# Another written-out order for a BigBird-attention and MLP kernel: loads, transposes and the mask's table at other places

## The chip, the cores and the metric

The kernel runs on one core of one Trainium2 chip. Its time is the device time of one execution in microseconds (us); the time of the kernel before is the median of three runs.

## The reference

Attention over 4 batches, 8 heads, 768 positions and head size 64, with a block mask (blocks of 32: neighbours, the first and last block, three drawn blocks for each row), and behind it a residual MLP that first mixes positions and then channels:

```python
scores = scale * q @ k.T                     # per batch and head, 768 x 768
scores = where(mask, scores, -1e9)           # block mask from sampled_blocks
attn = softmax(scores); x = attn @ v         # heads side by side: (4, 768, 512)

a1 = alpha1 * x + beta1
u  = x + lam * (w_tok @ a1)                  # mix of positions
a2 = alpha2 * u + beta2
ch = maximum(a2 @ w_ch1, 0) @ w_ch2          # 512 -> 2048 -> 512
out = u + lam * ch
```

## The kernel before

Nothing in this kernel is scheduled by a planner at build time. The whole order of work is a string, `ORDER`, of 1,589 words (line 49 and following). Each word is a kind, a number and sometimes an argument; the loop at the end calls the function registered for the kind. `pin_order` then ties the instructions of each engine to the order in which they were issued, and `bank_order` adds the waits that the eight banks of PSUM need. So every engine works strictly in the order of the words that fall to it, and a word that waits holds up everything behind it on its engine:

```python
for word in ORDER.split():
    kind = word[: next(j for j, c in enumerate(word) if c.isdigit())]
    n, _, arg = word[len(kind) :].partition(":")
    step[kind](int(n), *args)
```

Attention runs over 16 pairs of heads, p = 0 to 15, and each pair over 9 units of 1,024 scores (n = 9p to 9p + 8). The words of the attention are:

- `lq`, `lk`, `lv` p: POOL issues the load of a pair's q, k or v (192 KB as moved), which go through six shared buffers. From pair 7 on, the load first waits for a flag that a word `F` sets on DVE.
- `cq`, `ck`, `cv` p: copies of a loaded tile into the layout needed, on ACT (`:a`) or DVE (`:d`); they free the load's buffer.
- For the pairs 0 to 4, `H` transposes a head's q and k on TensorE, and `hq`, `hk` copy the result. From pair 5 on, `tq` and `tk` p let SP issue a DMA transpose of q or k (L593).
- `q` n:j: the scores of unit n on TensorE (L624 for the first five pairs, L634 after); `e` n: the exponential on ACT (L645); `m` n: the mask by a minimum on DVE, from pair 5 on; `p`, `r` n: the values on TensorE (L661); `n`, `nt`: normalising on DVE (L709, L712).

For the first five pairs the mask is part of the contraction. For the others a table `maskT` is needed: `M0` writes 24 rows of it from a tile of the mask on DVE (L532), `N0` lets SP write these rows to memory, spread out (L538), and `O0` reads the table back in its final shape (L545).

The words of the MLP are:

- `lt` g: thirds of w_tok (384 KB each); `W`, `w`: its transposes on TensorE and their copies; `k`: the mix of positions (L763); `a`, `b`, `ah`, `bh`, `x`, `u`, `U`, `v` around it.
- `lw` g and `lx` g: the four quarters of w_ch1 and of w_ch2 (512 KB each); `lc`: the small vectors. w_ch2 takes the place in SBUF that w_tok had.
- `f` i:bank: one column group of the first half of the MLP on TensorE, four matmuls (L828) into a PSUM bank; `g` i: bias and relu out of that bank, on ACT or DVE (L842, L844).
- `S` g: scales an eighth of w_ch2 by lam, on DVE (L513); S0 and S1 need lx0, S2 and S3 lx1, S4 and S5 lx2, S6 and S7 lx3. `T`: sums of quarters of w_ch2 on DVE (L866).
- `A`, `h`, `o`: the second half (a scheme with seven products in place of eight); `V`, `Y`, `y`, `d`, `D`: the first half for the later batches; `P` scales w_ch1; `s`: stores.
- `z`: matmuls that fill time on TensorE and compute nothing.

All loads are issued by POOL, in the order of their words, and go through one DMA queue, q0; the DMA transposes and the mask's writes and reads are issued by SP, in the order of their words, and go through others (q1 in the profile).

Of the kernel before, what the change touches and what calls it, by code (L numbers as in the profile page):

```python
# [54 lines left out]
ck3:d q25:1 F22 w0:d lk5 p12 w5:d e25 p13 q19:3 n2 W4:4 e19 H6:0 F28 lx3 w4:d q22:1 hk6:d r13:1
q17:2 e22 L1 q20:3 hq6:d e17 q24:1 L0 r14 H7:0 e20 q18:2 ck4:d a0 lv3 r15 e18 r16 r17 lc5 b0 q23:3
e24 cv2:d k1:4 n3 lk6 e23 lx1 q21:1 cq4:d r22:1 F42 x1 H9:5 e21 lv6 q28:3 F38 a1 p18:4 lw0 e28 r23
F40 q26:1 b1 p19 e26 hk9:d p20 r24 p21 hq7:d r25 cq6:a q27:3 cv4:d hq9:d r26 lq7 e27 p22 q30:1 hk7:d
k0:5 lw3 n5 e30 lc4 L2 H8:0 F23 F32 x0 q35:3 lw1 hk8:a hq8:d q31:1 lw2 k3:5 n4 e35 lx2 cv3:d q29:0
# [8 lines left out]
g28:a f18:0 cq8:d cv5:d g13:a f22:5 cv7:d tq6 g16:d g6:a f21:2 g23:d g22:a f27:1 g18:a tk8 P3:d  # L68
g20:a g21:d f14:3 g27:a P2:d f29:2 tk7 g14:a F34 b4 lk11 f30:0 g29:d lk9 tq8 cq11:d q53:2 g30:a
q48:1 P4:d k9:1 e53 lk12 A8 A0 lv8 e48 q50:3 q46:2 x9 h0:0 lq10 e46 A9 A1 h14:1 e50 A4 q52:1 o0  # L70
q49:2 e52 q45:3 A2 h1 A10 e49 h2 o12 A11 e45 h15 m48 P0:a F27 m50 lq9 q51:1 q47:2 m49 p48:6 e47 k8:7
F43 m45 m46 e51 p49 p50 o1 q58:2 x8 q56:1 e58 nt16 h16 m51 e56 m52 q60:2 q59:3 h3 o13 e60 A3 p45:2
m58 e59 p46 h17 m53 u8:a m47 u9:a q57:2 q55:3 F36 o2 e57 p47 U4 o14 p51:3 m59 h4 ck11:a m56 p52 e55
p53 nt15 lk14 q63:2 nt17 h18 e63 o3 q64:1 m57 q54:3 e64 q71:2 m60 h5 o15 e54 p57:2 a5 p58 h6 e71 b5
p59 ck12:a m64 q70:2 q62:3 nt19 e70 h19 lk10 m71 e62 q69:1 m54 q61:2 h20 F47 A5 ck9:a m55 p54:6
cq9:a k11:7 lv11 o16 e61 o4 tq9 lq13 h7:1 x11 cq10:a m62 k10:0 tk9 e69 m61 lv9 p60:7 A6 q67:2 tq10
m69 p55 e67 p56 o6 q80:1 x10 p61 e80 p62 nt18 q66:2 h8 nt20 e66 m70 q78:1 ck10:a q68:3 a6 p69:0 e68
p70 lk13 h9 m66 b6 e78 p71 o7 q65:2 q76:3 m63 u10:a q75:1 e65 nt23 h10 m67 u11:a p63:0 cv8:d k12:4
e76 m65 U5 lq12 m68 p66:5 e75 p64 x12 p67 tk10 p68 o8 q81:3 nt22 q86:1 e81 p65 h11 nt21 e86 m75
q74:2 q73:3 a7 e74 k13:0 b7 e73 q72:1 x13 q77:2 o9 u12:a k14:0 u13:a m76 e72 U6 k15:6 x14 A7 e77  # L80
p75:0 p76 x15 q79:1 u14:a m72 q85:2 u15:a h12 m77 e79 U7 m73 p77 e85 q82:3 m80 q93:1 s5 h13 m78 e93
tq11 m79 p78:4 p72:5 m74 e82 p73 p79 tk11 o10 p80 p74 q84:1 P1:d q87:3 nt24 e84 s0 f37:1 m86 tk12
f35:5 e87 nt26 f39:2 ck13:d g35:a m84 lq14 f54:3 g37:a nt25 g39:a q89:2 cv9:d q95:3 e89 q94:0 g54:d
lv10 f38:2 m82 e95 f32:3 P5:d P7:d f34:4 g32:a P6:d f48:5 e94 ck14:d m85 lk15 p84:3 a8 g34:a q83:3
q98:0 e83 p85 cq12:d f47:4 F44 F41 cv11:d tq12 lv15 m81 e98 p86 f61:6 g47:d lv12 g48:a p81:7 m83
q92:0 g61:a q88:2 b8 g38:a p82 f49:6 nt28 e92 m98 f36:2 e88 g49:d f63:3 m89 g36:a q106:0 m87 q91:2
g63:a p83 f51:6 e106 nt27 f56:2 m88 g51:a p87:3 cq13:d e91 f41:7 V0 m94 p88 g56:a q90:0 q96:2 cv10:d
g41:a m93 f52:2 e90 m92 p89 f57:6 m95 g52:a f53:7 e96 V2 p93:2 nt29 g57:a q97:0 q99:2 cq14:d e97
f33:3 m96 tq14 m91 p94 e99 p95 k16:6 m97 tk13 g33:a nt31 g53:a q104:0 m90 q102:1 s2 e104 q103:2 x16
f62:7 s1 a9 e102 tq13 p90:6 p91 p96:0 m99 p92 g62:a p97 nt30 tk14 p98 e103 f60:1 nt32 q113:1 m104  # L90
g60:a q100:2 s3 q105:3 e113 m102 s4 f59:0 b9 k17:1 e100 m113 F45 m103 lq15 e105 f55:2 x17 f44:3 lv14
g59:a m100 g55:a q108:2 m106 q107:0 lv13 e108 q101:3 m105 k18:2 a10 e107 p102:4 f50:5 m108 e101 x18
p99:0 p100 b10 g50:a f58:1 m101 g44:a p103 g58:a q131:3 m107 q115:1 p105:5 A20 e115 f45:1 A12 p106
e131 p104 A16 p101 p107 nt33 g45:a q112:1 k21:6 nt34 e112 nt35 q116:0 A21 q111:1 e116 q130:2 a11
k19:7 e111 x21 h35:0 x19 e130 m111 f43:1 m131 k20:2 g43:a A17 cv12:a o30 q109:2 V4 q114:3 e109 f40:1
A22 f42:3 m112 g40:a f46:4 e114 x20 m109 p111:1 h36 g46:a m114 g42:a cq15:d q110:2 m116 q133:1 e110
q126:3 b11 h37 m115 u16:a p112 ck15:a p113 p114:4 nt37 p115 e126 p116 tk15 p108:5 m130 p109 h28:1
e133 o31 A13 tq15 h38 cv14:a nt38 o24 u20:a q129:1 m110 q127:3 h29 A18 e127 A23 p110 e129 h30 nt36
o32 u21:a q134:2 A19 q132:1 e134 q128:3 o25 h39 m126 u17:a m129 q117:2 e128 U8 h31 m133 u18:a o33
p129:6 u19:a p130 m128 p131 e117 U9 k23:7 a12 e132 h40 o26 U10 nt43 cv15:a h41 x23 b12 u23:a q138:1  # L100
m127 q118:2 q119:3 e118 o34 h32 V5 cv13:a h21:0 m132 e119 m134 k25:4 o27 e138 k24:5 A14 x25 q142:1
o18 q143:3 A15 p126:4 p127 e143 x24 h33 m118 e142 p132:5 m117 h34 m138 p133 o28 p134 q141:1 nt44
q139:3 e141 p117:1 m143 p128 p118 h22 e139 nt42 m119 q135:1 a14 q125:2 e135 k22:6 b14 u24:a p119
e125 x22 h23 m141 u22:a q120:1 nt39 q140:2 e120 q137:3 U11 m142 k29:1 o19 e140 V1 k28:2 m125 u25:a
x29 e137 p141:3 U12 p142 m120 p143 h24 u29:a m139 m140 q123:2 q121:3 o20 e123 p138:1 x28 p139 h25
nt47 e121 Y8 p140 o21 u28:a q124:1 q122:2 e124 q136:3 nt46 U14 h26 Y9 e122 V3 y112:1 p120:2 m121
y126:3 e136 y113:4 Y10 h27 d126:a m135 d112:a m122 y127:5 y119:6 o22 y114 d119:a y120:7 d130 s6 y128
d113:a V6 y121 s10 d127:a p135:0 y115 Y11 d120:a y133:5 d116 d114:a y129 d123 y122 d133:a y117:4
m136 D116:a p121 y116 d128:a d117 p122 y131:7 d121:a nt40 p136 y118 d131 y130 y140:2 m124 d129:a
y123 m137 y135 d115:a y132 d118 d140:a y124:3 d132 p137 d122:a y141:1 d124 D117:a y142 y161:4 d144  # L110
d141:a y162:6 m123 y125 d161:a y134:1 nt45 d134:a y143 d165 y154:7 D130:a y136 d137 d154:a y147:6
d125 p123:0 D124:a p124 a15 D132:a p125 y156 d135:a y163 b15 d147:a y155:1 y148:3 nt41 d142:a y149
d158 y137 y145:0 d151 d148:a k31:1 d145 d162:a V7 d155:a y144 a13 y138:3 d136:a y150 d143:a y157
d138 y164 y146 b13 d149:a y152:2 x31 D158:a y139 D137:d k26:5 u31:a d146 D144:a D145:d d152 d156:a
y159:0 d139 k27:1 d163:a D165:d D151:a x26 D123:a y166:3 x27 y151 y153 d166 u27:a k30:1 D138:d u26:a
d153 D166:a U13 d159 y167 D139:a D125:d y165 D152:a d167 y160 h42:5 D118:d D167:a D131:d d160 D153:a
# [962 lines left out]
```

## Time and profile before

| | |
|---|---|
| median of three runs | 292.2 us (292.03 to 292.49) |
| the profiled execution | 291.82 us, span 290.1 us from the first to the last instruction |
| mean granted TensorE clock | 1.00 |
| TensorE busy | 283.9 us (98%), 3,538 matmuls |
| DVE busy | 263.8 us (91%) |
| ACT busy | 234.0 us (81%) |
| POOL busy | 53.3 us (18%) |
| DMA | 30.95 MB, 107 GB/s over the span |

The profile is of one execution. Rows of a timeline give a start, a duration, the engine, the code line, the operation with the tile written and the tiles read, and in square brackets how long the engine had stood idle before and what released it. Slices show tenths of busy time in 40 equal parts of the span, about 7.25 us each. The names in the rows are those of the program: `rel` a casted q or k, `qx` and `kx` the transposed ones, `eT` a unit's exponentials, `wtk` w_tok, `w1b` and `w2b` the MLP's weights, `hts` the MLP's hidden values, `x_sb` the running result, `psum` a PSUM bank.

### The profile page before, as it was taken

The page shows a single profiled execution, that of the slowest core. Times are in us where ns is not written, and L with a number is a line of the kernel's source. Part 1 is how long each engine was busy: PE and PEld are TensorE (multiplying, and loading weights), DVE is VectorE, ACT ScalarE, POOL GpSimd, SP SyncE. Part 2 cuts the span into 40 slices and gives each one's busy share as a digit, 9 for nine tenths or more (in the row PEclk, how much of TensorE's full clock was granted, in tenths as well). Part 3 has the DMA queues.
Part 4 walks back from the last instruction along what each step waited for, and adds up shares of the span by engine and source line. Part 5 has one row for each costly group of instructions (what it writes and reads, how often), then busy time and mean ns, then how long its engine had stood idle before and what let it go on. Part 6 is the DMA issues. An engine that isn't in the chain of part 4 may idle for free.

```text
span 290.1 us, 8529 instructions
## 1 busy us (share of the span) xinstructions
PE 283.9 (98%) x3538; PEld 213.6 (74%) x3538; DVE 263.8 (91%) x595; ACT 234.0 (81%) x350; POOL 53.3 (18%) x102
## 2 busy tenths in 40 slices
PE   8899999999999999999999999999999999999995
...
DVE  5689997689999999999999999999999998699983
...
PEclk9999999999999999999999999999999999999999
DMA  6999999999983498499278002404110140330014
GB/s 161 189 246 210 195 211 194 203 165 176 168 115 30 53 140 118 74 164 135 27 186 146 7 2 57 85 3 47 37 75 0 19 112 0 148 145 1 2 42 177
DMA packets 47927, 30.95 MB, mean 107 GB/s; under 512 B 28792, under 2 KB 43984, under 8 KB 47888
## 3 DMA queue, kind: packets, MB, share of 16 engines
...
HBM read 31.16 MB, written 6.88 MB: 131 GB/s over the span
## 4 chain that ended last, share of the span: by engine, by line
PE 87%; ACT 5%; DMA 4%; DVE 2%; issue 1%; POOL 0%; ACTq 0%
PE psum L907 26%; PE psum L997 13%; PE psum L828 12%; PE psum L661 11%; PE psum L763 11%; PE psum L634 9%; PE psum L624 4%; DMA wtk<-in_moe_w_tok_dram 3%; ACT hts L842 2%; ACT eT L645 2%; DMA k2f<-in_k_dram 1%; PE psum L806 1%; PE psum L355 1%; DVE a1p L733 0%; ACT rel L419 0%
## 5 line engine op out<-in xcount | busy, mean ns | idle before, releaser
L645 ACT ACTIVATE eT<-psum 128x1024 f16<-128x1024 f32 (+1 forms) x145 | 140.4, 1028 | 9.3 <-PE psum L634 5.4
L655 DVE TENSOR_TENSOR eT<-eT,maskT 128x960 f16<-128x960 f16 x99 | 61.2, 650 | 0.0
L907 PEld LDWEIGHTS <-hts 128*128 128x128 bf16 x480 | 45.1, 98 | 8.5 <-issue 2.1
L661 PEld LDWEIGHTS <-eT 128*128 128x128 f16 x1152 | 44.4, 97 | 8.3 <-issue 1.7
L661 PE MATMUL psum<-vext,eT 128*128 128x65 f16 x1152 | 48.5, 193 | 0.0
L828 PE MATMUL psum<-uT,w1b 128*128 128x384 bf16 (+1 forms) x256 | 45.9, 327 | 0.1
L1023 ACT ACTIVATE snap<-psum,b1t 128x384 f32<-128x384 f32 x44 | 23.7, 581 | 17.7 <-PE psum L997 13.4
L763 PE MATMUL psum<-a1p,wtokT 128*128 128x128 bf16 x576 | 36.8, 219 | 0.2 <-DVE x_sb L772 0.2
L763 PEld LDWEIGHTS <-wtokT 128*128 128x128 bf16 x576 | 33.2, 98 | 4.1 <-DVE x_sb L772 0.8
L907 PE MATMUL psum<-w2t,hts 128*128 128x256 bf16 x288 | 35.8, 273 | 0.0
L866 DVE TENSOR_TENSOR x_sb<-x_sb,psum 128x256 f32<-128x256 f32 (+1 forms) x61 | 30.7, 514 | 4.7 <-PE psum L907 4.5
L828 PEld LDWEIGHTS <-w1b 128*128 128x128 bf16 x256 | 23.0, 98 | 16.1 <-ACT b1t L419 0.9
L842 ACT ACTIVATE hts<-psum,b1t 128x384 bf16<-128x384 f32 x53 | 29.2, 602 | 0.9 <-PE psum L828 0.5
L634 PE MATMUL psum<-qx,kx 64*128 64x256 bf16 x396 | 29.8, 272 | 0.0
L866 DVE TENSOR_TENSOR hts<-snap,psum 128x384 bf16<-128x384 f32 x48 | 24.7, 547 | 2.7 <-PE psum L997 2.3
L624 PE MATMUL psum<-qx,kx 88*128 88x512 bf16 (+1 forms) x120 | 25.8, 326 | 1.3 <-ACT eT L645 1.0
L907 PE MATMUL psum<-w2b,ss 128*128 128x256 bf16 x192 | 24.6, 273 | 0.0
L907 PE MATMUL psum<-w2b,hts 128*128 128x256 bf16 x192 | 24.4, 273 | 0.0
L634 PEld LDWEIGHTS <-kx 64*128 64x128 bf16 x396 | 15.2, 94 | 8.4 <-issue 3.5
L907 PEld LDWEIGHTS <-ss 128*128 128x128 bf16 x192 | 18.0, 98 | 3.8 <-issue 0.6
L772 DVE TENSOR_TENSOR x_sb<-x_sb,psum 128x384 f32<-128x384 f32 x32 | 17.4, 546 | 1.0 <-PE psum L763 0.8
L997 PEld LDWEIGHTS <-w1b 128*128 128x128 bf16 x128 | 12.1, 98 | 6.6 <-DVE hts L866 0.3
(103 smaller groups left out, 362.5 us busy)
## 6 DMA issues: line engine op xcount, KB each, us to landing
...
```

Of the source, the lines that this page charges most:

```text
L624: nc.tensor.matmul(t[:, f : f + w], kx[h][0:KC, ts(jt, P)], qx[h][0:KC, c : c + w], start=True, stop=True,)
L634: nc.tensor.matmul(t[:, (2 * a + j) * TH : (2 * a + j + 1) * TH], kx[h][r, ts(2 * g + j, P)], qx[h][r, ts(th, TH)], start=True, stop=True,)
L645: nc.scalar.activation(eTs[n][:, c], t[:, c], AF.Exp, bias=EXPB, scale=SCALE)
L655: nc.vector.tensor_tensor(out=e, in0=e, in1=mask, op=ALU.min)
L661: nc.tensor.matmul(ops[key][:, t * VW : t * VW + D + 1], eTs[n][:, c : c + P], vext[n // NU % NV][:, a, jt, 0 : D + 1], start=(first and z ...
L763: nc.tensor.matmul(t[:, j, :], wtokT[:, s, ts(3 * g + j, P)], a1p[p][:, s, :], start=(s == 0), stop=(s == NT - 1),)
L828: nc.tensor.matmul(hps[i][:, 0:w], w1b[:, dk, ts(f, P)], uT[b][:, dk, hf * HS : hf * HS + w], start=(dk == 0), stop=(dk == 3),)
L842: nc.scalar.activation(hts[kk][:, f, :], t[:, 0:HS], AF.Relu, bias=b1t[:, f : f + 1], scale=1.0)
L866: nc.vector.tensor_tensor(out=out, in0=in0, in1=in1, op=op)
L907: nc.tensor.matmul(cps[b, q][:, side * HD : (side + 1) * HD], lhs[:, nk, :], rhs[:, nk, :], start=(z in (0, 6) and nk == 0), stop=(nk == H ...
L997: nc.tensor.matmul(chains[key], lhs[:, dk, ts(f, P)], rhs[:, dk, :], start=(z in (0, 1, 5) and dk == 0), stop=(dk == 1), skip_group_check= ...
L1023: nc.scalar.activation(dst, t, act, bias=bias, scale=1.0)
```

## The change

Only the string `ORDER` is another. It holds the same words, in another order; some words have another bank, and some copies change the engine: four `cv` and three `D` go from DVE to ACT, three `ck` and two `g` from ACT to DVE. The functions are unchanged; the new string is two lines longer, so that code lines in the changed kernel are two higher than those named here.

The new order comes from a search that counted the DMA transposes as landing later. The word that writes the mask's table, `M0`, stands behind `r25` and `q34`, the values of a unit of pair 2; before, it stood behind `x7` and `u1`, ahead of `p36`.

The core of the diff, from the first words to the words that finish the first half's first column groups (the rest of the string differs in the same manner, but for its last words):

```diff
-lv0 lk1 lq1 q0:0 lt1 q3:1 cq0 e0 lq2 q2:2 H1:6 lk2 e2 hq1:d q1:0 lv1 z480:7 hm0 z480:7 e1 hk1:d
-cv0:d q5:2 ck1:d e3 lq3 q4:0 p0:6 lt0 e4 p1 p2 lt2 q6:1 cq1:d e5 p3 lk3 p4 H2:7 H3:0 lc2 e6 hk2:d
-q7:2 lc0 F35 W2:1 hq2:d e7 lc1 q8:1 hq3:d r4:7 lk4 r5 w2:d e8 q9:2 cq2:d r6 F24 ck2:d lv2 r7 e9 n0
...
-W1:4 e16 q15:0 hq5:d p9:5 e15 p10 hq4:d q13:1 F21 cq3:d W0:7 F46 w1:d e13 lv4 q14:0 p11 W5:4 e14
...
-ck5:a x3 lq5 q32:3 ck6:d e31 k2:4 lk7 a2 e29 lx0 b2 p27:5 q34:1 x2 lv7 p28 u0:d e34 p29 p30 u3:d p31
...
-ah6 e38 q40:3 ah7 k5:4 cv6:d e37 bh7 lk8 bh6 q36:1 cq7:d e40 x5 k7:0 lv5 F33 u4:d e36 B0 k6:1 x7
-u1:a M0 p36:0 v1:a F39 u5:d p37 p38 x6 q41:1 u6:d U0:1 e41 q43:2 u7:d U2:6 S6 p39 e43 U3:7 v0:d
-q44:1 v2:a v3:d p40 q42:2 F26 S7 r40:1 r41 e44 f0:6 f6:7 e42 f3:2 g0:a f5:3 cq5:d g3:d f1:6 tq5 lq11
-g5:a F31 n8 r42 f8:2 N0 r43 g8:d f17:0 tk5 f24:3 r44 g24:d f9:2 tk6 S1 f11:3 g9:a g1:d f15:4 ck7:a
-S4 f25:2 g11:a n9 f19:5 F30 S3 f12:1 S2 f2:3 g12:a S0 f31:6 g19:a S5 g15:a f26:1 T0 g2:a f10:4 f4:3
-g10:a T1 f28:5 g26:a f20:4 g31:a T2 g25:a f16:1 ck8:a f7:2 a4 g4:a f23:6 g17:a T3 O0 f13:3 g7:a tq7
...
+lv0 lq1 lk1 lt1 lk2 q0:0 q3:1 lq2 cq0 e0 z480:4 lt2 H1:4 q1:3 e3 hq1:d lt0 q2:0 hk1:d lc0 e1 lv1
+hm0 cv0:d q6:1 F22 e2 lc1 q4:2 cq1:d lc2 p0:6 p1 e4 q7:0 lv2 p2 ck1:d e6 lk3 q5:2 p3 lq3 H2:7 e7
+z480:2 hq2:d H3:2 p4 e5 hk2:d q8:0 W2:3 n0 e8 r4:7 q9:2 F27 w2:d r5 W3:6 e9 hk3:d q10:0 ck2:d r6
...
+e13 H5:7 lc5 w4:d q15:1 hq5:d W0:0 e15 q12:2 w5:d z480:1 W1:1 hk5:d e12 q17:1 lx3 cv1:d q18:3 w0:d
...
+hq6:d r25 q34:0 M0 q32:2 b1 r26 e32 p20 cv3:d k1:2 n5 lv6 e34 p21 x1 p22 q30:2 F23 F21 cq4:d q35:0
+u1:d e30 lq5 k2:7 L2 n4 lx2 e35 q28:1 a2 q29:2 e28 q27:0 F42 x2 k3:6 e29 ck4:d F37 b2 lq6 q31:1
+e27 x3 H8:7 lw0 H9:4 hq8:d lx1 e31 k4:5 F34 u2:d hk8:a F28 u3:d p27:6 p28 hq9:d q33:0 ck5:a r31:7
...
+ah6 U0:6 q36:0 n7 q38:1 e36 ck6:d U1:7 u4:d lv5 k5:4 ah7 e38 lx0 bh6 q40:0 bh7 x5 k7:5 e40 cv4:d
+cv6:d lk8 k6:4 v1:a x7 lq8 v0:d u5:a q41:0 x6 u7:a q43:1 cq6:d e41 p36:4 cq5:d lv7 r40:5 u6:d p37
+tq5 U2:6 e43 F31 S7 r41 lk7 U3:7 q39:0 v2:a N0 v3:d p38 q44:1 tk5 f2:6 e44 f3:7 S3 e39 tk6 f10:2
+S6 r42 g2:a r43 cq7:d r44 g3:a f6:3 lq9 cv5:a p39 g6:d p40 f15:0 g10:a lq10 n9 f0:1 f8:5 g0:d
+f18:2 g8:a S4 f13:1 g15:a S1 f5:3 g18:a S0 f22:0 S2 f17:2 F46 g5:d F41 S5 f1:5 f11:3 T0 f7:6 g11:a
+F26 f26:7 T1 g22:a f19:3 g26:a ck7:d f21:0 T2 g1:a f24:7 g7:a F35 F32 f16:5 F33 n8 g21:a cv7:a
+f20:6 a4 g19:a f4:0 O0 g13:d f9:3 tq7 g4:a T3 f23:4 g9:a tq6 f30:0 F43 P0:a P2:d ck8:d f14:1 b4
...
```

More of the change, by code (lines that the diff above doesn't have):

```diff
@@ L55 @@
[L55 to L59, printed above, removed]
-ck5:a x3 lq5 q32:3 ck6:d e31 k2:4 lk7 a2 e29 lx0 b2 p27:5 q34:1 x2 lv7 p28 u0:d e34 p29 p30 u3:d p31
@@ L67 @@
-g10:a T1 f28:5 g26:a f20:4 g31:a T2 g25:a f16:1 ck8:a f7:2 a4 g4:a f23:6 g17:a T3 O0 f13:3 g7:a tq7
[L68 to L116, printed above, removed]
@@ new lines @@
+z480:2 hq2:d H3:2 p4 e5 hk2:d q8:0 W2:3 n0 e8 r4:7 q9:2 F27 w2:d r5 W3:6 e9 hk3:d q10:0 ck2:d r6
+hq3:d e10 r7 lq4 q11:2 cq2:d r8 w3:d e11 lv3 q14:1 n1 H4:0 lw3 W4:1 e14 hq4:d q13:2 lw1 W5:6 hk4:d
+e13 H5:7 lc5 w4:d q15:1 hq5:d W0:0 e15 q12:2 w5:d z480:1 W1:1 hk5:d e12 q17:1 lx3 cv1:d q18:3 w0:d
+e17 p9:4 w1:d lk4 p10 r13:5 L0 p11 e18 q16:0 F30 L1 p12 p13 e16 q25:1 a0 q23:3 r14 e25 n2 r15
+q19:0 ck3:d e23 r16 F24 b0 q22:1 lv4 cq3:d r17 e22 k0:4 lc4 n3 lk5 e19 F47 F38 q26:3 x0 q24:1
+cv2:d e26 H7:4 a1 lk6 q20:0 H6:5 e24 lw2 hq7:d p18:6 r22:7 r23 hk6:d p19 e20 q21:1 hk7:d r24 e21
@@ new lines @@
+tq5 U2:6 e43 F31 S7 r41 lk7 U3:7 q39:0 v2:a N0 v3:d p38 q44:1 tk5 f2:6 e44 f3:7 S3 e39 tk6 f10:2
[3 more added lines that the diff above has]
+f20:6 a4 g19:a f4:0 O0 g13:d f9:3 tq7 g4:a T3 f23:4 g9:a tq6 f30:0 F43 P0:a P2:d ck8:d f14:1 b4
+g16:a tk8 f25:3 F40 g17:d lk13 g23:a f12:5 g24:d lk10 g14:a tk7 P3:d f28:2 cq8:d g30:a lk9 P1:d
@@ new lines @@
+f31:4 g25:d g20:a tq8 lv8 f27:7 g12:a g31:d f29:3 g27:d g28:a h0:6 g29:a P4:d A0 q45:0 q49:1 e45
+q52:2 A8 h14:7 A4 e52 k8:0 A9 e49 o12 A10 h15 cq9:a o0 x8 q48:1 A1 k9:1 lk11 e48 A5 u8:a q51:2 A2
+q53:1 e51 h1 x9 m48 e53 q50:0 m49 h2 e50 m52 q47:1 m51 q46:2 u9:a p48:0 A3 tq9 e46 p51:1 p49 m45
+p52 h16 e47 o1 U4 m50 q58:2 m53 q60:1 e58 h3 o13 A11 e60 p50 m58 q59:2 p53 e59 o2 q57:1 nt17 h17
+e57 cq10:d nt16 lk12 h4 m47 ck10:a o14 q56:0 q54:1 m57 lv9 e56 q55:2 h18 m46 e54 o3 p45:0 p46 m59
+p47 e55 p57:1 nt15 q63:1 p58 e63 m54 p59 q61:2 nt19 h5 e61 m55 a5 q68:0 q71:1 e68 q70:2 h6 b5 o15
@@ new lines @@
+e70 p54:0 p55 m56 k11:1 e71 F45 m61 o4 ck11:a q62:2 q65:1 m68 p56 e65 k10:6 lq11 x11 m60 e62 h19
+nt18 ck9:a x10 q69:0 q67:1 m63 e69 q66:2 tk9 lq12 h7:6 m62 cv8:a m69 p60:0 tq10 p61 e67 m65 h20
+lq14 o6 e66 m70 p62 h8 A6 u11:a m66 q75:1 u10:a q64:2 e75 nt20 h9 U5 o16 e64 p63:0 m67 p66:1 s3
+p69:7 o7 q78:1 q73:2 m71 e78 p70 h10 m64 cv9:a a6 p71 p67 e73 p64 lv10 b6 p68 p65 nt22 q86:1 q76:2
+o8 e86 k13:1 nt23 nt21 e76 q80:1 x13 k12:7 e80 a7 q72:0 b7 q79:2 e72 q85:1 m80 h11 x12 e79 A7
+k15:0 o9 u12:a k14:1 u13:a m78 e85 U6 x15 p78:7 x14 u15:a q74:2 q77:1 m72 u14:a q84:0 h12 e84 m79
@@ new lines @@
+U7 m76 p79 e74 p80 m73 h13 tk10 m75 e77 q82:0 m74 p75:4 s5 e82 p72:5 o10 p76 p73 m77 s1 q89:1
+cq11:a q87:0 m84 s2 p74 e89 p77 lk14 tq11 nt24 f38:6 P7:d e87 f48:5 nt25 s4 f55:2 P5:d g48:a tk11
+P6:d f51:3 g38:a m89 g55:a q83:0 m82 q81:2 f34:2 m86 e81 f62:6 cq12:d nt26 g34:a lq13 f54:4 g51:a
+m81 e83 f60:5 ck13:d g54:d lv11 f52:7 g60:a ck12:d g62:d tk12 lv13 q91:0 g52:a q88:1 m85 q93:2 e91
+f36:6 cq14:d tq12 a8 lq15 p84:7 e88 p85 p81:0 m83 p86 e93 f57:1 nt28 p82 m91 g36:a q96:1 q95:2
+g57:d f61:7 e95 m87 f53:1 b8 cv10:a f49:6 m88 g53:a lv15 p83 g49:d p87:4 e96 p88 p89 nt27 f42:5
@@ new lines @@
+g61:a nt29 q92:0 g42:a a9 q97:1 q94:3 e97 k16:4 V4 e94 ck14:d f39:5 m97 lk15 f50:2 e92 cq13:d x16
+lv12 k17:3 b9 g50:a m93 g39:a q90:0 x17 q100:3 e90 q102:2 m95 f58:2 m94 e100 f37:3 m90 p93:0 g37:a
+m92 p94 p95 e102 f56:1 nt31 p90:3 m96 g56:a p91 p92 g58:a cv11:d q98:2 m100 q105:0 lv14 e98 tq14
+q106:3 V0 k19:2 nt30 e106 tk13 f47:4 m98 e105 x19 p96:5 p97 m106 p98 tq13 g47:a q107:1 nt32 q101:0
+e107 q99:3 cv12:d f63:4 tk14 m102 e99 f41:5 a10 f59:2 s0 g63:a m99 e101 f32:3 m107 k18:4 b10 g32:a
+g59:a q103:0 g41:a x18 q111:3 q104:1 A20 e111 f33:4 m105 k21:5 e104 A16 m101 p105:6 e103 f35:7
@@ new lines @@
+m111 p106 g33:a x21 p107 g35:a q110:0 nt35 q113:1 e110 q112:2 A21 k20:7 m103 e113 f43:6 A17 u18:a
+p99:0 m104 e112 p102:1 p103 m110 p100 p104 g43:a x20 p101 q108:1 m113 q109:2 e108 h28:6 nt34 nt33
+e109 h35:7 m112 ck15:a q129:0 o30 q115:1 A12 f40:4 e115 tk15 a11 f46:5 g40:a f44:2 o24 e129 A13
+f45:3 A18 g46:a h29 u21:a m115 g44:a A22 q116:0 u17:a q134:2 V1 p111:2 e134 p112 p113 b11 h36 e116
+m109 h37 nt37 g45:a m108 q130:0 A23 q114:1 e130 q133:2 o31 h30 A19 e114 h38 m116 cq15:a m130
+q131:0 o32 p108:2 u16:a tq15 o25 p109 cv14:a h39 m114 m134 u20:a p110 p114:3 U10 nt36 p115 p116
@@ new lines @@
+h31 V5 cv15:a nt38 U8 k23:2 e133 o26 a12 e131 h32 o33 q139:2 o27 q128:0 e139 h40 m129 x23 e128 h33
+b12 m131 h41 m133 q126:0 m139 q117:1 e126 q127:2 m128 h34 o34 e127 p129:0 o28 p130 p131 e117 k24:1
+nt43 m126 cv13:a q132:1 q138:2 m127 e132 q118:3 k22:0 V2 e138 m117 h21:2 x24 u19:a m132 p126:1
+e118 U9 p127 x22 p128 o18 q119:2 u23:a p132:0 nt42 e119 k25:3 A14 u24:a m118 q140:2 u22:a q141:3
+m119 h22 e140 U11 x25 p133 m138 u25:a p134 h23 e141 nt44 U12 a14 q124:0 q136:2 e124 q120:3 p117:3
+o19 p118 m140 h24 e136 A15 p119 e120 o20 q125:0 m141 q143:2 h25 e143 b14 nt39 p138:6 e125 p139
```

44 lines of the change are left out of this document (28 added, 16 removed).

## The prediction

> **What bounds the kernel now.** I read the page first: busy time, then the slices.
>
> ```profile
> PE 283.9 (98%) x3538; PEld 213.6 (74%) x3538; DVE 263.8 (91%) x595; ACT 234.0 (81%) x350; POOL 53.3 (18%) x102
> PE   8899999999999999999999999999999999999995
> DVE  5689997689999999999999999999999998699983
> PEclk9999999999999999999999999999999999999999
> DMA  6999999999983498499278002404110140330014
> ```
>
> TensorE is busy 283.9 of 290.1 us, at the full granted clock throughout. Both orders hold the same words, so TensorE has the same matmuls to do, and the last words of the two orders are alike. So a new order can give back at most 290.1 − 283.9 = 6.2 us, and can lose without limit wherever TensorE is made to wait. The digits say where to look: the first slices (8, 8), where TensorE does wait now, and the stretch from 50 to 75 us (slices 7 to 10), where DVE reads 9 or 8 and the DMA engines 9 for most of it, and where the new order moves most. The question is therefore not what work costs but whether anything arrives late.
>
> Second view: the timeline of the first 27 us, TensorE's weight loads beside POOL, which issues all loads.
>
> ```profile
> 9.37 0.56 PEld L624 LDWEIGHTS <-kx 88*128 88x128 bf16 x5 [1.23 <-ACT eT L645]
> 9.99 0.72 POOL L437 DMA_DIRECT2D q<-in_q_dram  x1 [2.01 <-DVE vext L421]
> 10.70 1.11 POOL L460 DMA_DIRECT2D wtk<-in_moe_w_tok_dram  x2
> 13.28 0.39 PEld L496 LDWEIGHTS <-wtk 128*128 128x128 bf16 x6 [0.71 <-DMA wtk<-in_moe_w_tok_dram]
> 19.07 0.39 PEld L496 LDWEIGHTS <-wtk 128*128 128x128 bf16 x6 [0.30 <-issue]
> 25.94 0.33 PEld L624 LDWEIGHTS <-kx 88*128 88x128 bf16 x3 [0.57 <-ACT eT L645]
> ```
>
> In square brackets stands the idle time before a row and what ended it. The weights of the token mix (lt0, lt2) were issued at 10.70, since POOL first stood 2.01 us in front of lq3, which needed a buffer that a cast on DVE (L421) had to free. Their transposes W then came to TensorE before the data.
>
> Third view: the timeline of the stage in which the first MLP half begins (words f, L828), with SP and POOL, and the landing times of two loads.
>
> ```profile
> 53.78 3.43 PE L828 MATMUL psum<-uT,w1b 128*128 128x385 bf16 x20
> 55.67 0.36 DVE L421 COPY rel<-q 128x768 bf16<-128x768 bf16 x1 [1.62 <-DMA q<-in_q_dram]
> 56.10 1.32 SPq L593 DMA_TRANSPOSE qx<-rel  x1
> 57.47 0.83 SPq L538 DMA_DIRECT2D mask_rows<-maskT  x1
> 58.41 7.66 SPq L593 DMA_TRANSPOSE kx<-rel  x2
> 44.36 0.77 POOL L485 DMA_DIRECT2D w2b<-in_moe_w_ch_dram  x1
> DMA to landing us min/median/max: 14.8/14.8/14.8
> ```
>
> The third row begins a burst on SP's queue: tq5, the mask's table (N0), tk5, tk6. What released it is the cast cq5 above it (55.67), which had waited 1.62 us for lq5. The last two rows are lx0, the last quarter of w2 to be loaded: issued at 44.36, landed 14.8 later, at 59.1.
>
> **The change, part by part.**
>
> Early loads. The new order asks for lt2 and lt0 ahead of lq3 and puts W2 and W1 later among the units. The waits 0.71 and 0.30 should go. The 0.57 before q24 goes too, since the units are staggered otherwise there. The 1.23 after the first exp stays, as nothing can be put there. 0.71 + 0.30 + 0.57 = 1.6 is the most; POOL's buffers stay as scarce, and I take 0.9 as the nearest estimate, 0 as the other end.
>
> The mask's table. M0 moves from behind x7 to behind q34, one operation on DVE:
>
> ```profile
> L532 DVE TENSOR_SCALAR maskT<-qx 24x768 f16<-24x768 bf16 x1 | 0.4, 351 | 0.0
> ```
>
> 0.35 us on DVE in either place, beside TensorE's work, hence 0. If its cover were gone it would cost 0.35. Its DMA, N0, remains behind tq5 on SP's queue, so its place in time is set by tq5 and not by M0.
>
> Engine letters. Four casts cv go from DVE to ACT and three relu words D from DVE to ACT; three ck and two g go the other way.
>
> ```profile
> L419 ACT COPY vext<-v 128x768 f16<-128x768 f16 x4 | 3.3, 833 | 0.0
> L421 DVE COPY vext<-v 128x768 f16<-128x768 f16 x12 | 4.6, 388 | 0.0
> L1033 ACT ACTIVATE hts<-hts 128x384 bf16<-128x384 bf16 x28 | 13.0, 515 | 0.8 <-DVE hts L866 0.7
> L1035 DVE TENSOR_SCALAR hts<-hts 128x384 bf16<-128x384 bf16 x20 | 4.9, 252 | 0.0
> ```
>
> ACT gets 4 × 0.83 + 3 × 0.52 = 4.9 and gives three copies of the same size (2.5) and two g; that is about +1.2 over the whole span. DVE stays within 0.2 of what it had. ACT has 56 us free by the first row of the page: 0.
>
> The order of the loads, which decides. In the new order lq5 has less ahead of it: two loads of q, k or v, one of w1 and two of w2, that is 2 × 0.197 + 3 × 0.524 = 1.97 MB (192 KB and 512 KB each). What the loads' queue q0 moved:
>
> ```profile
> q0 software_dynamic: 8261, 9.54, 104.6%
> q0 software_dynamic: 8928, 10.12, 105.7%
> q0 software_dynamic: 690, 0.61, 125.2%
> q1 hardware_dynamic: 891, 0.30, 69.9%
> q0 software_dynamic: 544, 0.39, 74.7%
> ```
>
> These are the DMA view's rows (packets, MB, share of the engines) for 0 to 53.1 us, 0 to 56, 50 to 53, and, the last two, 58.7 to 64. Undisturbed, q0 moves 0.61 MB in 3 us, 0.20 MB/us, so lq5 is there some 9.7 us sooner, at about 46, and cq5 no longer waits for it. SP's burst then starts when DVE reaches cq5, whose place is eight words of TensorE before the first f: q39, q44, U2, U3, r40, r41, p37, p38. The chain of waits prices them:
>
> ```profile
> 50.28 0.44 PE psum L624 x3
> 51.66 0.34 PE psum L806 x6
> 52.00 0.25 PE psum L661 x8
> 58.34 1.30 PE psum L828 x8
> ```
>
> 2 × 0.44 for q, 2 × 0.34 for U, 4 × 0.25 at most for p and r: 2.4 to 2.6 us. The first f of the new order (f2) stands at before's 53.78, less p39 and p40, which move behind it (12 matmuls of the third row's kind, 0.37), less the early 0.9: 52.5. So cq5 falls at about 50.1 and tq5 at 50.5, where it was at 56.10.
>
> That is 5.6 us earlier, and it collides with loads. In before the burst's packets begin at about 58.7, 2.6 us after its first issue. From there q0 falls to 0.39 MB in 5.3 us, 0.074 MB/us, about a third. That hurt nobody, because lx0 had all been sent: its end is at 10.10 MB of the stream (20 loads of q, k and v, three thirds of w_tok, three vectors' rows, eight loads of w), a volume that q0 passed at 55.9. In the new order the burst's packets begin at 53.1, with 9.54 MB moved and 0.56 MB of lx0 and its neighbours to come, for the volume ahead of lx0 is the same in both orders. At 0.074 MB/us that takes 7.6 us: sent at 60.7. From volume to landing it took 59.1 − 55.9 = 3.2 in before, so lx0 lands at 63.9 and not at 59.1.
>
> Who waits: S1, S0 and S2 scale w2 on DVE, the first two being lx0's halves, and g5:d stands behind them there. Then f11:3 waits for the bank that g5 empties.
>
> ```profile
> 61.06 0.62 DVE L844 TENSOR_SCALAR hts<-psum,b1t 128x384 bf16<-128x384 f32 x1
> 62.20 0.19 DVE L709 RECIPROCAL rcp<-psum 128x6 f32<-128x6 f32 x1
> 62.42 0.56 DVE L712 TENSOR_TENSOR x_sb<-psum,rcp 128x384 f32<-128x384 f32 x1
> 63.51 1.89 DVE L513 TENSOR_TENSOR w2b<-w2b,lam_bcb 128x1024 bf16<-128x1024 bf16 x3
> 65.43 1.22 DVE L866 TENSOR_TENSOR w2t<-w2b 128x2048 bf16<-128x2048 bf16 x1
> ```
>
> 63.9 + 1.89 + 0.62 = 66.4. f11 is due after thirteen f (two in 1.30, so 0.65 each), r42 to r44 and p39, p40: 52.5 + 8.45 + 0.75 + 0.37 = 62.1. TensorE waits about 4.4 us (66.5 with the hand-over). Had lx0 landed at 59.1, g5 would end at 61.6 and f11 would wait for nothing. With q0 at half of its rate, 0.10 MB/us, lx0 is sent at 58.7, lands at 61.9, g5 ends at 64.4: 2.3. I take the third, which the same burst showed here, on the same queues. [...]
>
> A second wait follows. lk7 is four loads of 192 KB (0.79 MB) behind lx0. Half of it at the slow rate (5.3 us) and half at the full one (1.9) lands it at 60.7 + 7.2 + 3.2 = 71.1. DVE comes to ck7 after S5 (0.63), T0 and T1 (1.22 each) at 69.6, so it stands 1.5. Behind it are ck7 (a copy, 0.37), T2 (1.22) and n8 (0.19 + 0.56), and f23:4 needs n8's bank: 71.1 + 2.3 = 73.4, against ten f after 66.5, 73.0. So 0.4, between 0 and, with all of it slow (10.7 us), 3.9.
>
> What an earlier burst gains: the readers of its transposes, the scores of the pairs 5 and 6, stand behind all words f in both orders, long after it, so nothing.
>
> Sum against the profiled execution of 291.8 (290.1 and 1.7 around it): −0.9 + 4.4 + 0.4 = +3.9. The median of the runs is 0.4 above that execution, 292.2, so 296.1.
>
> **The rivals.**
>
> A, faster: the loads keep pace. Either lx0 goes out at its old rate, because the burst's packets meet other loads than I place there, or lq5 comes no earlier and the burst stays at 56. Then only the early waits go: 292.2 − 0.9 = 291.3. For it: f11 has 0.5 us to spare at lx0's old landing. Against it: the 0.074 MB/us, in which any delay of more than 0.5 us costs. DVE's rows tell against it too:
>
> ```profile
> 60.00:70.00 10.00, 9.96 (x62) 5.49 (x60) 9.83 (x17) 7.79 (x20) 0.00 (x0) 1.00 1.25 179
> ```
>
> (stretch, length, then busy time of PE, its weight loads, DVE, ACT, POOL.) DVE is busy 9.83 of 10 us there, so what is lost in a wait on DVE is not made up behind it. Where the delay is just about 1.4 us, early gain and late loss cancel: the same as before.
>
> B, slower still: the second wait has its full size, since tq7, tq6 and more transposes follow the burst: −0.9 + 4.4 + 3.9 = +7.4, 299.6. It decides if q0 stays at a third beyond 61 us.
>
> C: the clock. A 512-column matmul took far longer at the start than in the mean of its later kind:
>
> ```profile
> L315 PE MATMUL psum<-warm 128*128 128x512 bf16 x6 | 2.7, 630 | 0.0
> L624 PE MATMUL psum<-qx,kx 88*128 88x512 bf16 x60 | 20.0, 379 | 0.5 <-ACT qx L394 0.3 <-ACT eT L645 0.2
> ```
>
> If a wait of 4.4 us put TensorE back into that state for as long as it lasted, the work in it would take 630/379 = 1.66 times as long: 4.4 × (1 − 1/1.66) = 1.8 more, 297.9. Against it: the longest wait of before is 1.23, so the trace cannot show whether a longer one does this, and the granted clock reads 9 even in the first slice. [...]
>
> **How the numbers follow.** A change of 0.2% (0.6 us) is about what a measurement of this kernel can tell from none. The first case, lx0's delay with a small second wait, has 0.52: 296.1, its own range 293.6 (half rate, no second wait) to 297.9 (half way to B). B has 0.12, C 0.08, A 0.20, and cancelling 0.08. Faster is A alone, 0.20; same 0.08; slower 0.72. The range runs from A's 291.1 to 299.8, just past B.
>
> **What would show it.** In the changed profile: tq5 issued near 50.5; q0 down to a third from 53; lx0 landing at 63 to 65; S1 or S0 on DVE with 3 us or more of idle time ended by the DMA of w2b; and a gap before f11's matmuls, with the waits for w_tok at 13 and 19 us gone. I am wrong if lx0 lands by 60, or if another wait than S1's holds TensorE.

## The result, and the profile after

| | before | after |
|---|---|---|
| median | 292.25 us (22 runs, 291.63 to 295.12) | 293.74 us (22 runs, 292.17 to 295.81) |
| ratio to before | | 1.0046, 95% interval 1.0027 to 1.0065 |
| span of the profiled execution | 290.1 us | 291.2 us |
| mean granted clock | 1.00 | 1.00 |

The change makes the kernel slower by 0.46%, some 1.4 us. The side of the forecast was right, the size was not: 3.9 us were forecast. By the two signs that the prediction named, it was wrong in its mechanism: lx0 landed before 60 us, and another wait than S1's held TensorE, as the rows below show.

The page of the changed kernel, the rows that answer to those shown of before:

```profile
PE 284.0 (98%) x3538; PEld 214.2 (74%) x3538; DVE 264.3 (91%) x594; ACT 234.8 (81%) x351; POOL 52.4 (18%) x102
PE   8999999998899999999999999999999999999995
DVE  5699999687999999999999999999999998879983
PEclk9999999999999999999999999999999999999999
DMA  6999999999983379289977014114300025140014
```

TensorE's second slice has become a 9, and the tenth and eleventh (65 to 80 us) have become 8. Those are the two sides of the account: something gained at the start, more lost in the stage in which the MLP's first half runs. The busy times by stretches (stretch, length, then PE, its weight loads, DVE, ACT, POOL, clock, DMA) put sizes to them; first before, then after:

```profile
10.00:20.00 10.00, 9.62 (x145) 7.13 (x144) 7.75 (x20) 9.75 (x11) 6.10 (x10) 1.00 1.18 208
20.00:30.00 10.00, 9.82 (x149) 7.41 (x147) 9.37 (x25) 9.91 (x12) 5.12 (x8) 1.00 1.24 235
70.00:80.00 10.00, 9.94 (x86) 6.17 (x84) 9.41 (x21) 9.58 (x20) 4.75 (x10) 1.00 1.12 157
```

```profile
10.00:20.00 10.00, 10.00 (x153) 7.99 (x152) 7.74 (x20) 9.73 (x12) 4.45 (x7) 1.00 1.15 234
20.00:30.00 10.00, 10.00 (x167) 7.90 (x166) 9.44 (x25) 10.00 (x12) 6.43 (x10) 1.00 1.18 217
60.00:70.00 10.00, 8.87 (x55) 5.09 (x54) 6.96 (x17) 6.21 (x16) 0.00 (x0) 1.00 1.17 180
70.00:80.00 10.00, 8.84 (x69) 5.30 (x67) 9.88 (x22) 6.98 (x13) 4.25 (x9) 1.00 1.03 158
```

From 10 to 30 us TensorE has no idle time left (0.56 before). From 60 to 80 us it stands 2.29 us where it stood 0.10. DVE, which I had read as full in 60 to 70 us (9.83), is busy 6.96: it waits. The timeline shows for what. DVE first, then TensorE's idle rows behind it:

```profile
57.95 2.49 DVE L515 TENSOR_TENSOR w2b<-w2b,lam_bcb 128x1024 bf16<-128x1024 bf16 x4
67.17 0.36 DVE L423 COPY rel<-k 128x768 bf16<-128x768 bf16 x1 [2.87 <-DMA k<-in_k_dram]
67.45 1.22 DVE L868 TENSOR_TENSOR w2t<-w2b 128x2048 bf16<-128x2048 bf16 x1
68.89 0.56 DVE L714 TENSOR_TENSOR x_sb<-psum,rcp 128x384 f32<-128x384 f32 x1
...
69.50 1.47 PE L830 MATMUL psum<-uT,w1b 128*128 128x384 bf16 x8 [1.13 <-DVE x_sb L714]
71.22 2.13 PE L830 MATMUL psum<-uT,w1b 128*128 128x385 bf16 x12 [0.24 <-DVE hts L846]
74.03 2.12 PE L830 MATMUL psum<-uT,w1b 128*128 128x384 bf16 x12 [0.68 <-DVE hts L846]
76.39 0.82 PE L830 MATMUL psum<-uT,w1b 128*128 128x384 bf16 x4 [0.24 <-DVE hts L846]
```

The first row holds S4, S1, S0 and S2: no idle time stands before them, so lx0 was there. The second is ck7, which waited 2.87 us for lk7. In the kernel before, lk7 was asked for ahead of lx0 and landed at 56.7, and ck7 ran on ACT, at 61.25; the change moved the load behind lx0 and the cast to DVE. T2 (third row) and n8 (fourth) stood behind it, and f23, which needs the bank that n8 empties, came 1.13 us late at 69.50. The three shorter gaps follow from the same lateness of DVE: in the experiments in which lk7 comes in time they go, or shrink to 0.24 in all. Together: 1.13 + 0.24 + 0.68 + 0.24 = 2.29.

SP's burst, then POOL's issue of lx0 with its time to landing, and that of lk7 (issued at 50.81):

```profile
49.83 1.32 SPq L595 DMA_TRANSPOSE qx<-rel  x1
51.20 0.82 SPq L540 DMA_DIRECT2D mask_rows<-maskT  x1
52.14 7.65 SPq L595 DMA_TRANSPOSE kx<-rel  x2
```

```profile
45.80 0.77 POOL L487 DMA_DIRECT2D w2b<-in_moe_w_ch_dram  x1
DMA to landing us min/median/max: 11.8/11.8/11.8
...
DMA to landing us min/median/max: 16.3/16.3/16.3
```

The burst is where it was forecast: 49.8, beside 50.5. But lx0 landed at 57.6, sooner than before, and lk7 at 67.1. What the two queues moved (packets, MB, share), from 0 to 54 us, 54 to 56, and 60 to 63:

```profile
q0 software_dynamic: 8627, 9.87, 105.0%
q0 software_dynamic: 318, 0.29, 104.8%
q1 hardware_dynamic: 323, 0.08, 50.6%
q1 hardware_dynamic: 284, 0.43, 52.8%
q0 software_dynamic: 279, 0.20, 49.9%
```

When the burst's packets began, at about 54, 9.87 MB of the loads had gone, and lx0 needed 0.23 more. From then until about 65 us the two queues sent nearly the same number of packets (318 and 323, 279 and 284 in the rows shown). Beside the transposes' small packets (0.08 MB in 323, some 250 bytes each) the loads kept 0.145 MB/us; beside the mask's write (0.43 MB in 284, 1.5 KB each) they kept 0.07. lx0 met the first kind for 1.6 us. lk7, four loads behind, met both.

### The profile page after: what moved, and what is told of

It is laid out like the page before. It is cut to its first block, busy times and chain, and to the rows that moved or that the text cites. A ratio compares the mean times of both kernels' runs of the same rounds, so it can differ in the third digit from the quotient of the medians.

```text
span 291.2 us, 8514 instructions
## 1 busy us (share of the span) xinstructions
PE 284.0 (98%) x3538; PEld 214.2 (74%) x3538; DVE 264.3 (91%) x594; ACT 234.8 (81%) x351; POOL 52.4 (18%) x102
## 4 chain that ended last, share of the span: by engine, by line
PE 88%; DMA 6%; DVE 4%; issue 1%; ACT 0%; POOL 0%; DVEq 0%
PE psum L909 26%; PE psum L999 13%; PE psum L663 12%; PE psum L765 11%; PE psum L636 9%; PE psum L830 8%; PE psum L626 6%; DMA k<-in_k_dram 6%; PE psum L317 2%; PE psum L357 1%; DVE w2t L868 1%; PE psum L498 1%; DVE rel L423 1%; DVE hts L846 0%; DVE x_sb L774 0%
## 5 line engine op out<-in xcount | busy, mean ns | idle before, releaser
L647 ACT ACTIVATE eT<-psum 128x1024 f16<-128x1024 f32 (+1 forms) x145 | 138.9, 1027 | 8.4 <-PE psum L636 6.0
L657 DVE TENSOR_TENSOR eT<-eT,maskT 128x960 f16<-128x960 f16 x99 | 61.9, 653 | 0.0
L663 PEld LDWEIGHTS <-eT 128*128 128x128 f16 x1152 | 42.8, 97 | 7.9 <-issue 1.5
L663 PE MATMUL psum<-vext,eT 128*128 128x65 f16 x1152 | 46.6, 193 | 0.0
L909 PE MATMUL psum<-w2t,hts 128*128 128x256 bf16 x288 | 34.9, 273 | 0.0
L844 ACT ACTIVATE hts<-psum,b1t 128x384 bf16<-128x384 f32 x51 | 28.2, 585 | 2.7 <-PE psum L830 2.2
L626 PE MATMUL psum<-qx,kx 88*128 88x512 bf16 (+1 forms) x120 | 25.0, 326 | 0.9 <-DVE qx L589 0.7
```

Source lines behind the costliest of these rows:

```text
L626: nc.tensor.matmul(t[:, f : f + w], kx[h][0:KC, ts(jt, P)], qx[h][0:KC, c : c + w], start=True, stop=True,)
L647: nc.scalar.activation(eTs[n][:, c], t[:, c], AF.Exp, bias=EXPB, scale=SCALE)
L657: nc.vector.tensor_tensor(out=e, in0=e, in1=mask, op=ALU.min)
L663: nc.tensor.matmul(ops[key][:, t * VW : t * VW + D + 1], eTs[n][:, c : c + P], vext[n // NU % NV][:, a, jt, 0 : D + 1], start=(first and z ...
L844: nc.scalar.activation(hts[kk][:, f, :], t[:, 0:HS], AF.Relu, bias=b1t[:, f : f + 1], scale=1.0)
L909: nc.tensor.matmul(cps[b, q][:, side * HD : (side + 1) * HD], lhs[:, nk, :], rhs[:, nk, :], start=(z in (0, 6) and nk == 0), stop=(nk == H ...
```

## The experiments

All ratios are to the kernel before, from runs on the same chip. Theory K: what costs is ck7's wait, through its place in DVE's order.

**The cast behind n8.**

```diff
-... g26:a ck7:d f21:0 T2 g1:a f24:7 g7:a F35 F32 f16:5 F33 n8 g21:a cv7:a
+... g26:a f21:0 T2 g1:a f24:7 g7:a F35 F32 f16:5 F33 n8 ck7:d g21:a cv7:a
```

> In the changed kernel DVE stood 2.87 us in ck7:d for lk7 (landed 67.15), and T2 and n8, which frees the bank of f23, stood behind it. Here ck7:d stands behind n8; nothing else is moved. Theory K (the late load costs through this one queue position): n8 ends at about 66.4, f23 finds its bank free, TensorE's four gaps between 69 and 77 us (1.13, 0.24, 0.68 and 0.24, together 2.3) go, and the time is 2.0 to 2.3 us below the changed kernel, about 291.5, so 0.6 to 0.8 below the kernel before. Rival R (DVE has too much work in this stretch, and its idle 2.87 us are beside the point): only the first gap goes, and the others stay, 1.1 us below the changed kernel, about 292.6.

Measured: 291.38 us, ratio 0.9979 (0.9965 to 0.9993). The load is as late as ever, but the wait behind it holds nobody:

```profile
65.70 0.56 DVE L714 TENSOR_TENSOR x_sb<-psum,rcp 128x384 f32<-128x384 f32 x1
67.15 0.36 DVE L423 COPY rel<-k 128x768 bf16<-128x768 bf16 x1 [0.89 <-DMA k<-in_k_dram]
...
71.97 2.12 PE L830 MATMUL psum<-uT,w1b 128*128 128x384 bf16 x12 [0.43 <-DVE hts L846]
74.33 0.82 PE L830 MATMUL psum<-uT,w1b 128*128 128x384 bf16 x4 [0.23 <-DVE hts L846]
```

By the two ratios to the kernel before (1.0046 and 0.9979) that is 2.0 us below the changed kernel, from one word's place on one engine. TensorE's idle time from 60 to 80 us fell from 2.29 to 0.66. Theory K holds. The 0.66 that is left is not the amount of work on DVE either: with the mask's write late (below), DVE does the same work and TensorE does not stand at all there. Here lk7 is still late, and ck7 still holds DVE for 0.89 us.

**The burst held back.**

```diff
-... r25 q34:0 M0 q32:2 ...
+... r25 q34:0 q32:2 ...
...
-tq5 U2:6 ... v2:a N0 v3:d ... tk5 f2:6 ... tk6 f10:2 ... S0 f22:0 S2 f17:2 ...
+U2:6 ... v2:a v3:d ... f2:6 ... f10:2 ... S0 f22:0 S2 M0 N0 tq5 tk5 tk6 f17:2 ...
```

> SP's burst of transposes and the mask's write (N0, tq5, tk5, tk6) is held back: M0 stands behind S2 on DVE, at about 60.4 us, and N0, which needs it, first on SP's queue. All loads keep their places. Theory C (the burst took half of the loads' queue): q0 keeps 0.20 MB/us until 61, lk7 lands at about 62 instead of 67.15, ck7 does not wait (DVE comes there at 64.3), the time is 2 us below the changed kernel, about 291.7. Rival P (lk7 is simply too far back in the order of the loads): it lands later than 64.3 still, and the time stays within 1 us of the changed kernel. In both, the readers of the transposes at 80 us and later still find them; if they do not, a new gap stands before the scores of pair 5.

Measured: 290.96 us, ratio 0.9958 (0.9943 to 0.9974). From 55 to 60 us the loads had the engines for themselves:

```profile
q0 software_dynamic: 1357, 1.00, 130.4%
```

That is 0.20 MB/us. lk7 landed at 61.4, nothing waited in ck7, and TensorE's gaps shrank to one of 0.24. So lk7's place among the loads is not too far back by itself: without the burst it comes in time. The burst could be some 11 us later without harm to the scores of pair 5.

**The mask's table back in its place.**

```diff
-... r25 q34:0 M0 q32:2 ... v1:a x7 lq8 ...
+... r25 q34:0 q32:2 ... v1:a x7 M0 lq8 ...
```

> Only M0, the word that writes the mask's table, is put back behind x7, where the kernel before has it. Prediction: nothing, within 0.3 us of the changed kernel (293.7), because N0 stands behind tq5 on SP's queue, and tq5 at 49.83 comes after M0's place in both. Rival: M0's 0.35 us now stand in DVE's queue just ahead of the stage that is bound by it: 0.3 to 0.4 us slower.

Measured: 293.15 us, ratio 1.0028 (1.0007 to 1.0049), against 1.0046 (1.0027 to 1.0065) of the changed kernel: the intervals overlap, and no difference is shown. The two ratios lie 0.5 us apart, so the forecast of nothing is not contradicted. In the trace of this run lk7 landed at 66.4 and ck7 stood 1.82 us; f23's gap of 1.13 was gone, and the three shorter ones (0.24, 0.68 and 0.24) stood. Whether M0 or the scatter of executions moved lk7 by 0.7 us, one trace cannot tell.

**lk7 three loads further ahead.**

```diff
-... cv6:d lk8 ... x7 lq8 ... cq5:d lv7 ... r41 lk7 ...
+... cv6:d lk7 ... x7 lk8 ... cq5:d lq8 ... r41 lv7 ...
```

> Four loads change places with each other: lk7 goes where lk8 stood, lk8 where lq8, lq8 where lv7, lv7 where lk7. The burst and every cast stay. Theory K: lk7 lands at about 59 instead of 67.15, ck7 does not wait, TensorE's gaps at 69 to 77 go: about 2 us below the changed kernel, 291.6. lv7 lands at about 67.2 instead of 65.8, where its cast on ACT is due at 66.1: ACT waits about 1 us with relu words behind it, which may give back up to 0.5. Rival R (too much work on DVE): 1.1 us or less below the changed kernel.

Measured: 291.62 us, ratio 0.9971 (0.995 to 0.9993). lk7 landed at 60.9 and ck7 did not wait. So with the burst where it is, the place of lk7 among the loads decides as well; it takes both, the burst and the late place, to make lk7 late. The load that took its place did what was feared, on ACT:

```profile
67.15 0.83 ACT L421 COPY vext<-v 128x768 f16<-128x768 f16 x1 [0.76 <-DMA v<-in_v_dram]
...
68.52 6.68 PE L830 MATMUL psum<-uT,w1b 128*128 128x385 bf16 x40 [0.64 <-ACT b1t L421]
```

**Two thirds of w_tok sooner, in the kernel before.**

```diff
-... lk2 e2 ... p0:6 lt0 e4 p1 p2 lt2 q6:1 ...
+... lk2 lt2 lt0 e2 ... p0:6 e4 p1 p2 q6:1 ...
```

> The kernel before with one thing moved: lt2 and lt0 (two thirds of w_tok) stand behind lk2, ahead of lv1 and lq3. Theory: the first f came 1.44 us sooner in the changed kernel (51.97 against 53.78 less 0.37 of work moved behind it), and the weights' earlier loads are the larger part of it, since the waits before W2 and W1 (0.71 and 0.30) and some of the start go: 0.7 to 1.0 us faster than the kernel before, about 291.3. Rival: the gain came from the stagger of the units among the other words, and the loads that are pushed back here (lv1, lq3) cost as much: within 0.3 us of the kernel before.

Measured: 293.73 us, ratio 1.0043 (1.0013 to 1.0074): a miss, in the wrong direction even for the rival. The wait of W2 stayed and two new ones came:

```profile
13.36 0.54 PE L496 MATMUL psum<-identb,wtk 128*128 128x128 bf16 x6 [0.20 <-DMA wtk<-in_moe_w_tok_dram]
20.29 0.65 PE L661 MATMUL psum<-vext,eT 128*128 128x65 f16 x16 [0.41 <-DVE vext L421]
21.94 0.54 PE L496 MATMUL psum<-identb,wtk 128*128 128x128 bf16 x6 [0.57 <-DVE qx L421]
```

W2 waits for lt1, which this edit does not move (it landed at about 13.3 here as in the kernel before). The wait before W1, which reads lt0, is gone, as expected (0.30 before). But lv1 and lq3, pushed back, now made their casts late. The changed kernel's gain at the start is not the loads' doing alone; that it is the new stagger of loads, units and transposes together is what is left, and no run isolates it.

**The burst early, in the kernel before.**

```diff
-... r26 lq7 ... x3 lq5 ... q36:1 cq7:d ... f5:3 cq5:d ...
+... r26 lq5 ... x3 lq7 ... q36:1 cq5:d ... f5:3 cq7:d ...
```

> The kernel before with lq5 and lq7 exchanged in the order of the loads, and cq5 and cq7 exchanged on DVE. SP's burst (tq5, N0, tk5, tk6) then starts at about 47.3 instead of 56.1, while lx0 is still on its way; TensorE's order, the other loads and casts stay. The prediction's step (a burst ahead of lx0 makes S1 late): with q0 at 0.145 MB/us beside the transposes' packets and 0.07 beside the mask's, as the changed kernel's trace has them, lx0 is sent at 59.7 instead of 55.9 and lands at 62 to 63 instead of 59.1; S1, due at 60.27, waits 1.5 to 2.5 us and the time is 1 to 2 us above the kernel before. At 0.074 throughout it would be sent at 64.5 and cost 6. Rival (the slack of lx0 covers it): no change. A loss ahead of the first f, from the last quarter of w1 (landed 52.1, due 53.8), would show as a gap there.

Measured: 299.15 us, ratio 1.0226 (1.0198 to 1.0254). Here is what I had forecast for the change, in full (DVE, then TensorE, then two stretches of 10 us):

```profile
65.02 0.69 DVE L513 TENSOR_TENSOR w2b<-w2b,lam_bcb 128x1024 bf16<-128x1024 bf16 x1 [4.83 <-DMA w2b<-in_moe_w_ch_dram]
...
67.79 7.49 PE L828 MATMUL psum<-uT,w1b 128*128 128x385 bf16 x35 [4.76 <-DVE x_sb L712]
...
60.00:70.00 10.00, 5.24 (x26) 2.52 (x24) 5.10 (x12) 2.78 (x8) 0.00 (x0) 0.88 1.22 143
70.00:80.00 10.00, 9.93 (x58) 5.68 (x57) 8.06 (x12) 8.76 (x24) 0.00 (x0) 0.94 0.71 131
```

With tq5 at 47.2, lx0 landed at 65.0 and S1 stood 4.83 us. The step is real when the burst comes early enough. The burst starts 2.6 us sooner here than in the changed kernel, but the two runs also differ in the order of the loads (lk7 is ahead of lx0 here), so that the start alone decides which load suffers is argued and not shown. It cost more than the 1 to 2 us expected, since lx0 landed 2 to 3 us later than I had it. The rest is the clock, which reads 0.88 and 0.94 in these stretches and 1.00 from 50 to 60 us. The first 35 matmuls behind the wait took 7.49 us (the row above); the next 41, up to 82.19 us, took 6.91, and at that rate 35 would have taken 5.90: by this estimate 1.6 us were lost. With TensorE's wait that is 4.76 + 1.6 = 6.4, and the span (296.2) exceeds that of before by 6.1.

**The mask's write behind the transposes.**

```diff
-tq5 ... v2:a N0 v3:d p38 q44:1 tk5 ... tk6 ... g19:a f4:0 O0 ...
+tq5 ... v2:a v3:d p38 q44:1 tk5 ... tk6 ... g19:a f4:0 N0 O0 ...
```

> The changed kernel with N0, the write of the mask's rows, moved on SP's queue from behind tq5 to just before O0, behind the transposes tk5 and tk6. Theory: the queues take turns packet by packet, so beside the mask's packets of 1.5 KB q0 had 0.07 MB/us (60 to 63 us), and beside the transposes' small ones 0.14; with the mask's write behind tk6, q0 keeps 0.14 for longer, lk7 lands 1 to 2 us sooner, at 65 to 66, and ck7's wait shrinks from 2.87 to 1 to 2; the time is 1 us below the changed kernel, 292.7. Rival (the share does not depend on what the other queue sends): no change, lk7 at 67. The mask's table is there some 3 us later for the pairs from 5 on; if that is too late, DVE waits before the first m.

Measured: 290.75 us, ratio 0.9943 (0.992 to 0.9965), 3.0 us below the changed kernel, where 1 was expected. The queues from 57 to 62 us, ck7, and the busy times of two stretches:

```profile
q0 software_dynamic: 976, 0.71, 90.9%
q1 hardware_dynamic: 988, 0.24, 37.3%
...
64.34 0.35 DVE L423 COPY rel<-k 128x768 bf16<-128x768 bf16 x1
...
60.00:70.00 10.00, 10.00 (x64) 5.99 (x62) 9.79 (x23) 6.79 (x17) 0.00 (x0) 1.00 0.95 157
70.00:80.00 10.00, 10.00 (x99) 6.96 (x98) 9.91 (x22) 8.78 (x16) 4.77 (x10) 1.00 1.25 169
```

Packets again one for one (976 and 988); beside transposes alone the loads keep 0.14 MB/us. lk7 landed at 64.1, 0.2 us before DVE came to it, so the whole wait went and not a part of it, and TensorE has no idle time left from 60 to 80 us. lk7 landed at 61.4 without the burst, at 64.1 beside the transposes alone and at 67.1 beside transposes and mask's write: each part costs it about 3 us, and the mask's write is the part that takes it past the 64.3 at which DVE comes to ck7.

**Both cures.**

```diff
-... v2:a N0 v3:d ... g26:a ck7:d f21:0 ... F33 n8 g21:a ... f4:0 O0 ...
+... v2:a v3:d ... g26:a f21:0 ... F33 n8 ck7:d g21:a ... f4:0 N0 O0 ...
```

> The changed kernel with both cures: N0 just ahead of O0 on SP's queue, and ck7:d behind n8 on DVE. With N0 late alone lk7 landed at 64.13, and DVE came to ck7 at 64.34, so there was nothing left to wait for. Theory: nothing more is to be had, the time is that of N0 late alone, 290.6 to 290.9, 1.4 to 1.7 us below the kernel before; what the second cure adds is cover for an execution in which lk7 lands later, so that the runs lie close together. Rival (the two cures hit different gaps): another 0.3 to 0.5 us below, about 290.3.

Measured: 291.0 us, ratio 0.9952 (0.993 to 0.9974). Nothing is added, as the theory has it. That the runs would lie closer together did not come true (290.01 to 292.35 in nine runs, against 290.34 to 290.91 in the four with the mask's write late alone).

## Why the prediction was right and wrong

The sum had three terms: −0.9 + 4.4 + 0.4. Measured on the profiled execution: about −1.0 to −1.4, 0, and +2.3, together +0.9 to +1.3, against 1.1 between the two spans. The largest term did not occur. That the side came out right all the same is luck: it rests on the smallest term, which was more than five times its forecast.

*The start.* −0.56 of idle time between 10 and 30 us and the first f at 51.97 instead of 53.41 (53.78 less the 0.37 moved behind it). In the seven executions that have the new order's start, the first f came at 51.88 to 52.32, so the gain is there each time and the size held roughly. The cause that I gave did not hold: I took W2's wait for one of lt2 and lt0, and W2 reads lt1; the two earlier loads alone make the kernel before slower.

*The burst's start.* Right: 49.83 for 50.5, and it took the loads' engines.

*lx0 late.* This is the step that failed: the prediction had S1 wait for lx0 and TensorE lose 4.4 us by it, and S1 did not wait at all. Its mechanism exists, as the burst moved early in the kernel before shows. Four figures were off, all to one side. The burst's packets began 4.1 us after its first issue instead of the 2.6 read off before. The loads were then 0.15 MB further on, because everything ran a microsecond sooner: 9.87 MB had gone by 54 us, where 9.54 by 53.1 was forecast. The rate beside the burst was 0.145 MB/us and not 0.074. And from volume to landing it took 2.0 us (55.6 to 57.6) and not 3.2. The rate weighs as much as the first two together: 0.56 MB at 0.145 would have put the landing at 60.2, and 0.23 MB at 0.074, from 54 us on, at 60.3, where 63.9 was forecast.

The rate of 0.074 was read rightly from the kernel before, but it does not carry over. There, from 59 to 62 us, the burst's packets were small ones too (0.13 MB in 519), and the loads still got only a third of their rate:

```profile
q1 hardware_dynamic: 519, 0.13, 83.3%
q0 software_dynamic: 280, 0.20, 63.8%
```

The two queues together moved 0.33 MB in these 3 us, and the counts are not equal; in the changed kernel the same kind of packets left the loads twice as much. Why before's own burst was so slow stays open. The half of the rate (0.10 MB/us) that I set beside the third was an estimate of mine. What the changed kernel's trace shows is nearly equal numbers of packets (392 against 394 from 57 to 59 us, 279 against 284 from 60 to 63) and no fixed share of the bytes: the loads kept 0.14 MB/us in the first stretch, beside packets of some 250 bytes, and 0.07 in the second, beside 1.5 KB.

*lk7 late.* Named, with the right chain (ck7, T2, n8, f23), and sized at 0.4 instead of 2.3. It was computed behind the first wait, where DVE would have reached ck7 at 69.6. Without that wait DVE came at 64.3, and lk7 at 67.1 was late by 2.87, although it landed 4 us sooner than I had it. The two terms are not to be added independently: the larger the first, the smaller the second. The same gap is in rival A, which dropped the first wait and did not work the second out again; it gave "faster", and the second wait turned it into "slower".

*The mask's table.* M0 itself: nothing, right. But of N0 I said only that its place is set by tq5. That was true and missed the point: where on SP's queue N0 stands is worth 3 us.

*Engine letters.* They were priced at 0 by the amount of work, and that amount was moved about as forecast. But a letter also sets the queue in which a word stands: ck7 is one of the three casts that went from ACT to DVE, and only there does it stand ahead of T2 and n8. No run puts ck7 back on ACT alone, so what this letter is worth stays open.

*The clock:* it stayed at 1.00 in the changed kernel, where the longest idle time of TensorE was 1.13 us. Rival C's condition, a wait of more than 4 us, came about only with the burst early in the kernel before (4.76 us), and there the clock cost 1.6 us by the estimate above; C had put it at 1.8.
